# Decoding three steps of channel weights during the value projections of the second and third batch

## Chip, cores, metric

The kernel runs on one core of a Trainium2 chip. The metric is device time in microseconds (us) of one execution; the median of several executions counts.

## What is computed

Four batches of 448 positions pass through three stages: an attention whose weights are a sigmoid, a gated projection (value projection, a convolution over five positions as the gate, output projection), and a mixer that first mixes positions (`w_tok1`, `w_tok2`) and then channels (`w_ch1`, `w_ch2`).

```python
scores = scale * np.matmul(q, k.transpose(0, 1, 3, 2)) - np.log(S)   # q, k, v: (4, 12, 448, 64)
x = np.matmul(1.0 / (1.0 + np.exp(-scores)), v)                     # then (4, 448, 768)
gate = 1.0 / (1.0 + np.exp(-gate_pre))      # gate_pre: conv over 5 positions, by channel
x = gate * (x @ w_val) @ w_out              # (768, 768) each
h = np.maximum(x.transpose(0, 2, 1) @ w_tok1, 0.0) @ w_tok2          # (448, 256), (256, 448)
u = x + h.transpose(0, 2, 1)
out = u + np.maximum(u @ w_ch1, 0.0) @ w_ch2                         # (768, 1536), (1536, 768)
```

All weights arrive as float64. The program on the host only lays arrays out; turning a weight into something that TensorE can multiply happens on the chip and is called decoding below.

## The kernel before

**Precision.** Every dense product is made of three matmuls. A weight is decoded into a high and a low part (`decode_ops`, L91), an activation is split the same way (`split`, L75: a copy on ScalarE, a subtraction on VectorE), and high times high, low times high and high times low are summed in PSUM. Decoding 128x768 weights (a "piece") takes six VectorE instructions (L98, L105, L108, L113, L119, L122) and two ScalarE instructions (L101, L130) on a raw tile of 768 KB.

**Stages.** `lead` (L79 of the inner block) runs attention, with the decoding of `w_val`, `w_out`, `w_tok1` and `w_tok2` between. Then for each of the four batches `dense_steps(b)` gives the steps of the value projections (`val`, six of 18 matmuls each, L320), of output projections, transposes and the first half of the position mixing (`outs`), and of the second half (`t1`, `t2`). The second half of a batch is run among the value projections of the next one. Then the channel stage: it has twelve steps `fc` for every batch, each of 18 matmuls into `psh` (`ch1`, L641) and 18 into the six accumulators `pso` (`ch2`, L660), so that TensorE runs `ch1(b, fc)`, `ch2(b, fc - 1)`, `ch1(b, fc + 1)` and so on. Between the two a relu split (`r`: L76 on ScalarE, L78 on VectorE) turns `psh` into the operand of `ch2`.

**Channel weights.** Step `fc` needs two pieces, one of `w_ch1` and one of `w_ch2` (`ld_ch`, `ch_parts`). They are decoded once and stay for all batches. Step 0 has a place of its own in the pool `p2a`. Steps 1 to 3 (`CHAN_HELD = 4`) lie in the twelve `w` tiles that held `w_val`, which are free once the last value projection has run. Steps 4 to 11 lie in a pool `p2r` on the right side, where `w_out`, `w_tok1`, `w_tok2` and the tiles of the position mixing were. The raw tiles of these loads are two, reused in turn, and are loaded by the queue of SyncE.

**Order.** Until the end of the position mixing the order is written by hand. `weave(steps, ops, share)` runs TensorE's steps and puts small operations (`ops`) between them, spread over a share of the steps. In the last batch, step 0 is decoded among the value projections, and steps 1 to 3 (48 operations) together with six `prep_split` (the split of the input of the channel stage) among `outs`, `t1` and `t2`, over a share of 0.95 (`OS_SHARE`). What follows, the decoding of steps 4 to 11 and the channel stage, is put in order by the scheduler of the language; the decoding has a low priority (`CHAN_LOW`). On each engine instructions run in the order in which they stand, so an instruction that waits holds up those behind it.

**Other queues.** GpSimd's queue (POOL) carries the stores of `x2T` to device memory (`uscr`, L378) and small memsets (L274) at each `x_back`; SyncE's queue (SP) carries `x_back` (loads of `xb`), the loads of `u` from `uscr`, and the raw loads.

Of the kernel before, what the change touches and what calls it, by code (L numbers as in the profile page):

```python
# [9 lines left out]
F32 = mybir.dt.float32  # L10
F32R = mybir.dt.float32r
# [4 lines left out]


CHAN_HELD = 4
CHAN_LOW = 600
OS_SHARE = 0.95  # L20

# [6 lines left out]
def tile_kernel(ctx, tc, qT, kT, v, w_val, conv_w, w_out, w_tok1, w_tok2, w_ch1, w_ch2, out):  # L28
# [31 lines left out]
    dram = ctx.enter_context(tc.tile_pool(name="dram", bufs=1, space=bass.MemoryType.DRAM))  # L60
    uscr = dram.tile([B, KD, P, S], F32, name="uscr")
    xscr = dram.tile([NPT, P, S], F32, name="xscr")

    def f(ap):
        return ap.bitcast(F32)
# [22 lines left out]
        load(raw)  # L88
        return raw

    def decode_ops(pool, n, raw, h_out, l_out, sum_out=None):  # L91
        w = raw[:, : 2 * n].rearrange("p (n t) -> p n t", t=2)
        lo, hi = w[:, :, 0], w[:, :, 1]
        t = {}

        def first():
            t["a"] = pool.tile([P, DC], I32, tag="dec_a", bufs=2, name="dec_a")[:, :n]
            nc.vector.tensor_scalar(out=t["a"], in0=hi, scalar1=0x7FFFFE00, scalar2=None, op0=ALU.bitwise_and)  # L98

        def rebase():  # L100
            nc.scalar.activation(out=t["a"], in_=t["a"], func=AF.Relu, scale=8.0, bias=exp_b)  # L101

        def rest():
            t["c"] = pool.tile([P, DC], I32, tag="dec_c", bufs=1, name="dec_c")[:, :n]
            nc.vector.tensor_scalar(out=t["c"], in0=hi, scalar1=0x1FF, scalar2=None, op0=ALU.bitwise_and)  # L105

        def join():
            nc.vector.scalar_tensor_tensor(  # L108
                out=lo.bitcast(F32), in0=lo.bitcast(U32), scalar=2.0**-32, in1=t["c"], op0=ALU.mult, op1=ALU.add
            )  # L110

        def sign():
            nc.vector.scalar_tensor_tensor(  # L113
                out=t["a"], in0=hi, scalar=-0x80000000, in1=t["a"], op0=ALU.bitwise_and, op1=ALU.bitwise_or
            )

        def power():
            t["e"] = pool.tile([P, DC], I32, tag="dec_c", bufs=1, name="dec_e")[:, :n]
            nc.vector.tensor_scalar(out=t["e"], in0=t["a"], scalar1=-0x800000, scalar2=None, op0=ALU.bitwise_and)  # L119

        def low():
            nc.vector.scalar_tensor_tensor(  # L122
                out=l_out, in0=lo.bitcast(F32), scalar=2.0**-20, in1=t["e"].bitcast(F32), op0=ALU.mult, op1=ALU.mult
            )
# [35 lines left out]
    def w_tile():  # L160
        return wval.tile([P, DM], F32R, tag="w", bufs=2 * KD, name="w")
# [382 lines left out]
    def weave(steps, ops, share=0.85):  # L544
        total = int(share * sum(n for n, *_ in steps))
        count, at, done = len(ops), 0, 0
        for n, fn, *hold in steps:
            fn()
            at += n
            due = done if hold else min(count, count * at // total, done + 4)  # L550
            while done < due:
                ops[done]()
                done += 1
        for fn in ops[done:]:
            fn()
# [2 lines left out]
    wch_t, r_b = {}, []  # L558
    rp = {}

    def ld_ch(fc, which):
        raw = rp["a"].tile([P, 2 * DC], I32, tag="raw", bufs=2, name="raw")
        if which == 0:
            nc.sync.dma_start(
                raw.rearrange("p (k m) -> p k m", k=KD),
                w_ch1[:, fc * P : (fc + 1) * P].bitcast(I32).rearrange("(k p) m -> p k m", p=P),
            )
        else:
            nc.sync.dma_start(raw, w_ch2[fc * P : (fc + 1) * P].bitcast(I32))
        return raw  # L570


    def ch_parts(fc, which, raw):
        if which == 0:
            if 0 < fc < CHAN_HELD:
                wch[fc] = [[w_tile() for _ in range(2)] for _ in range(2)]
            else:
                t = wch_t.pop(fc)
                wch[fc] = [[t[:, n, a] for a in range(2)] for n in range(2)]
        return decode_ops(rp["a"], DM, raw, *wch[fc][which])  # L580

    def wch_alloc(pool, fc):
        wch_t[fc] = pool.tile([P, 2, 2, DM], F32R, name=f"wch{fc}")

    def dec_ch(fc):
        for which in range(2):
            for fn in ch_parts(fc, which, ld_ch(fc, which)):
                fn()

    def ch_ops(fcs):
        pieces = [(fc, which) for fc in fcs for which in range(2)]
        raws = {}

        def load(n):
            if n < len(pieces):
                raws[n] = ld_ch(*pieces[n])

        load(0)  # L600
        load(1)
        ops = []
        for n in range(len(pieces)):
            cur = []

            def op(k, n=n, cur=cur):
                if k == 0:
                    cur += ch_parts(*pieces[n], raws.pop(n))
                cur[k]()
                if k == 7:  # L610
                    load(n + 2)

            ops += [lambda k=k, op=op: op(k) for k in range(8)]
        return ops

    def prep_load(b, j):
# [53 lines left out]
    with tc.manual_schedule():  # L670
# [23 lines left out]
        for b in range(B):  # L694
            val, outs, t1, t2 = dense_steps(b)
            if b:
                weave(val[0] + back1 + sum(val[1:], []) + back2, first if b + 1 == B else [])
            else:
                val = sum(val, [])
                for n in (12, 8, 4):  # L700
                    val.insert(n, (0, dec_step))
                weave(val, [])
                assert not (begun or raws or decs)
                dec.release()
                dn["late"] = tc.alloc_tile_pool(name="late", bufs=1, side="right", reuse_waits="tile")
            if b + 1 < B:
                weave(outs, post_ops(b + 1))
            else:
                os = outs + t1 + t2
            back1, back2 = t1, t2  # L710
            if b + 2 == B:
                xbp.release()
                rp["a"] = tc.alloc_tile_pool(name="p2a", bufs=1, side="left")
                wch_alloc(rp["a"], 0)
                first = ch_ops((0,))
        for j in range(KD):
            prep_load(0, j)
        ops = ch_ops(range(1, CHAN_HELD))
        for j in range(KD):
            ops.insert(6 * j + 6, lambda j=j: prep_split(0, j))  # L720
        weave(os, ops, OS_SHARE)
        psw.release()
    pso = tc.alloc_tile_pool(name="pso", bufs=1, space=bass.MemoryType.PSUM, reuse_waits="tile")
# [5 lines left out]
    for fc in range(KF - 1, CHAN_HELD - 1, -1):  # L729
        wch_alloc(rp["p"], fc)  # L730
    r_b += [rp["p"].tile([P, 2, S], F32R, tag="r", bufs=2, name="r") for _ in range(2)]
    with tc.high_priority(-CHAN_LOW):
        for fc in range(CHAN_HELD, KF):
            dec_ch(fc)
    seq = [(b, fc) for b in range(B) for fc in range(KF)]
    order = []
# [55 lines left out]
```

## Time and profile before

| | us |
|---|---|
| median of three executions | 743.78 (743.14 to 745.97) |
| the profiled execution | 744.49 |
| its span, first to last instruction | 742.7 |
| TensorE (PE) busy | 732.5 |
| VectorE (DVE) busy | 399.3 |
| ScalarE (ACT) busy | 255.9 |
| GpSimd (POOL) busy | 26.5 |

The stages in the span: attention to about 133 us, the dense part of the four batches to about 376 us, the channel stage to the end. PE's busy time covers nearly all of the span, and its granted clock was 1.000 throughout. The profiled execution took 1.8 us more than its span, and 0.7 us more than the median of the runs. A row's idle time is the time an engine waited before an instruction, and the arrow names what ended the wait.

### The profile page before, as it was taken

What the parts mean: (1) busy time and instruction counts of PE and PEld (TensorE: products, weight loads), DVE (VectorE), ACT (ScalarE), POOL (GpSimd) and SP (SyncE); (2) the same over time, 40 slices, a digit from 0 to 9 for tenths busy, and PEclk for the clock granted to TensorE, in tenths of its full rate; (3) what the DMA queues carried; (4) which work ended last, traced back from release to release, by engine and by line L of the source; (5) the groups of instructions that cost most, each with busy time, mean ns of one, the idle gap of its engine ahead of it and who ended that gap; (6) DMA issues with size and microseconds to landing.
All of it is one profiled execution on the core that took longest, in us unless ns stands there. A gap on an engine that the chain in (4) does not pass through costs nothing.

```text
span 742.7 us, 10706 instructions
## 1 busy us (share of the span) xinstructions
PE 732.5 (99%) x4360; PEld 605.5 (82%) x4360; DVE 399.3 (54%) x690; ACT 255.9 (34%) x379; POOL 26.5 (4%) x66
## 2 busy tenths in 40 slices
PE   8999999999999999999999999999999999999997
PEld 3344444899999999999988987899999999999997
DVE  1899675589449548866799998811022101220102
ACT  6898888244214213323434443300020000200000
POOL 0001100000000100000010000000000000000000
PEclk9999999999999999999999999999999999999999
DMA  9858996201111101315265555510015000240002
GB/s 288 264 155 237 274 290 208 75 13 51 50 37 51 63 4 59 123 51 186 95 195 173 169 171 170 164 60 1 1 46 178 1 0 1 63 149 0 1 1 74
DMA packets 48864, 77.79 MB, mean 105 GB/s; under 512 B 4000, under 2 KB 44208, under 8 KB 48816
## 3 DMA queue, kind: packets, MB, share of 16 engines
q1 hardware_dynamic: 45168, 62.86, 27.8%
q0 software_dynamic: 3216, 13.80, 5.3%
q8 instruction: 34, 0.56, 0.3%
q10 hardware_dynamic: 432, 0.46, 0.2%
q14 instruction: 14, 0.11, 0.0%
HBM read 61.96 MB, written 15.14 MB: 104 GB/s over the span
## 4 chain that ended last, share of the span: by engine, by line
PE 84%; DVE 10%; DMA 4%; ACT 1%; issue 0%; SPq 0%; ACTq 0%
PE psd L320 24%; PE pso L660 18%; PE psh L641 18%; PE pss L242 8%; PE psy L257 8%; PE pst L360 4%; PE pst L373 3%; DMA raw<-w_ch 3%; DVE dec_a L113 2%; DVE raw L108 2%; DVE wch L122 2%; PE pst L343 1%; DVE dec_e L119 1%; DVE dec_a L98 1%; DVE dec_c L105 1%; ACT ga L244 1%
## 5 line engine op out<-in xcount | busy, mean ns | idle before, releaser
L78 DVE SCALAR_TENSOR_TENSOR r<-psh,r 128x448 fp32r<-128x448 f32 x48 | 29.8, 623 | 210.1 <-ACT r L76 210.1
L660 PE MATMUL pso<-r,wch 128*128 128x448 f32 x648 | 139.0, 367 | 2.5 <-DVE r L78 1.6
L641 PE MATMUL psh<-us,wch 128*128 128x448 f32 x648 | 139.3, 367 | 1.3 <-ACT wch L130 0.7
L660 PEld LDWEIGHTS pso<-r,wch 128*128 128x128 f32 x648 | 121.5, 188 | 13.9 <-DVE r L78 2.0
L641 PEld LDWEIGHTS psh<-us,wch 128*128 128x128 f32 x648 | 121.4, 188 | 13.7 <-ACT wch L130 1.6
L76 ACT ACTIVATE r<-psh 128x448 fp32r<-128x448 f32 x48 | 25.9, 542 | 225.1 <-PE psh L641 224.9
L320 PE MATMUL psd<-gv,w 128*128 128x448 f32 x432 | 92.4, 369 | 0.0
L244 ACT ACTIVATE ga<-pss,bias_s 128x896 f32<-128x896 f32 x84 | 83.4, 1003 | 19.2 <-PE pss L242 18.6
L320 PE MATMUL psd<-xs,w 128*128 128x448 f32 x432 | 88.8, 365 | 0.0
L320 PEld LDWEIGHTS psd<-xs,w 128*128 128x128 f32 x432 | 81.0, 188 | 7.0 <-issue 0.7
L320 PEld LDWEIGHTS psd<-gv,w 128*128 128x128 f32 x432 | 80.2, 188 | 6.7
L242 PE MATMUL pss<-q,k 64*64 64x448 f32 x672 | 78.4, 538 | 1.0 <-ACT ga L244 0.7
L257 PE MATMUL psy<-ga,v 64*64 64x448 f32 x672 | 77.6, 536 | 0.0
L290 DVE SCALAR_TENSOR_TENSOR gate<-xb,cw,gate 128x448 f32<-128x448 f32 x96 | 65.7, 684 | 2.8
L242 PEld LDWEIGHTS pss<-q,k 64*64 64x64 f32 x672 | 25.7, 133 | 39.7 <-issue 29.0
L257 PEld LDWEIGHTS psy<-ga,v 64*64 64x64 f32 x672 | 25.7, 133 | 37.4 <-issue 35.9
L101 ACT ACTIVATE dec_a<-dec_a,exp_b 128x768 int32<-128x768 int32 (+3 forms) x43 | 36.8, 866 | 45.3 <-DVE dec_a L98 45.3
L113 DVE SCALAR_TENSOR_TENSOR dec_a<-raw,dec_a 128x768 int32<-128x768 int32 (+2 forms) x42 | 37.2, 887 | 19.9 <-ACT dec_a L101 19.7
L641 PE MATMUL psh<-us,w 128*128 128x448 f32 x216 | 46.7, 367 | 0.0
L660 PE MATMUL pso<-r,w 128*128 128x448 f32 x216 | 46.2, 366 | 0.2 <-DVE r L78 0.2
L660 PEld LDWEIGHTS pso<-r,w 128*128 128x128 f32 x216 | 40.5, 188 | 4.0 <-DVE r L78 0.6
L641 PEld LDWEIGHTS psh<-us,w 128*128 128x128 f32 x216 | 40.6, 188 | 3.7
(69 smaller groups left out, 625.5 us busy)
## 6 DMA issues: line engine op xcount, KB each, us to landing
raw<-w_ch SPq DMA_DIRECT2D x24, 768.0 KB, 4.4
v<-v SPq DMA_DIRECT2D x24, 224.0 KB, 6.1
uscr<-x2T POOLq DMA_DIRECT2D x24, 224.0 KB, 2.6
u<-uscr SPq DMA_DIRECT2D x24, 224.0 KB, 3.5
ur<-uscr SPq DMA_DIRECT2D x24, 224.0 KB, 3.4
out<-ur SPq DMA_DIRECT2D x24, 224.0 KB, 2.1
q<-qT SPq DMA_DIRECT2D x23, 224.0 KB, 4.7
k<-kT SPq DMA_DIRECT2D x22, 224.0 KB, 4.7
```

The source lines that it names most:

```text
L76: nc.scalar.activation(out=h_out, in_=src, func=AF.Relu if relu else AF.Copy)
L78: nc.vector.scalar_tensor_tensor(out=l_out, in0=src, scalar=0.0, in1=f(h_out), op0=ALU.max, op1=ALU.subtract)
L101: nc.scalar.activation(out=t["a"], in_=t["a"], func=AF.Relu, scale=8.0, bias=exp_b)
L113: nc.vector.scalar_tensor_tensor(out=t["a"], in0=hi, scalar=-0x80000000, in1=t["a"], op0=ALU.bitwise_and, op1=ALU.bitwise_or)
L242: nc.tensor.matmul(ps[cols, j, :S], k[rows, keys], q[rows], start=True, stop=True)
L244: nc.scalar.activation(out=a, in_=ps[:, :, :S], func=AF.Sigmoid, bias=bias_s, scale=QK_SCALE)
L257: nc.tensor.matmul(y_t[i + h][cols, :S], v_t[i][rows, c, cols], a[rows, j], start=c == 0, stop=c == NB - 1)
L290: nc.vector.scalar_tensor_tensor(out=acc, in0=x[:, t : t + S], scalar=w, in1=acc, op0=ALU.mult, op1=ALU.add)
L320: nc.tensor.matmul(ps[:, :S], w(a, kk), s[:, c, :], start=kk == 0 and n == 0, stop=kk == KD - 1 and n == 2,)
L360: nc.tensor.matmul(ps[:, :HALF], a, x[:, m], start=n == 0, stop=n == len(mm) - 1)
L641: nc.tensor.matmul(ps[:, :S], wch[fc][0][a][:, kk * P : (kk + 1) * P], us_t[b, kk][:, c, :], start=kk == 0 and n == 0, stop=kk == KD - 1 a ...
L660: nc.tensor.matmul(acc[j][:, :S], wch[fc][1][a][:, j * P : (j + 1) * P], r[:, c, :], start=fc == 0 and n == 0, stop=fc == KF - 1 and n == 2,)
```

## The change

Three steps of channel weights, `PRE = (2, 3, 4)`, are no longer decoded where the others are. A pool `pre` on the left side, in the place of the attention tiles, is opened after the first batch's value projections. The six pieces are decoded in it, three beside the second batch's value projections and three beside the third's (27 operations in each `weave`, over a share of 0.95). A ninth operation of each piece (`keep`) stores the high and low part to a scratch tensor `wscr` in device memory, by GpSimd's queue. Where steps 2 and 3 were decoded, `pre_load` loads them from `wscr` into `w` tiles (eight loads of 384 KB), and step 4 into its place in `p2r` (four loads), all by GpSimd's queue. The last `weave` holds 22 operations instead of 54, and the scheduler's part decodes steps 5 to 11 instead of 4 to 11. In `pre` the tiles `dec_a`, `pre0` and `pre1` exist once.

```diff
+PRE = (2, 3, 4)
...
+    wscr = dram.tile([len(PRE), 2, 2, P, DM], F32, name="wscr")
...
+    def ch_parts(pool, fc, which, raw):
+        if fc in PRE:
+            to = [pool.tile([P, DM], F32R, tag=f"pre{a}", bufs=1, name="pre") for a in range(2)]
+            ops = decode_ops(pool, DM, raw, *to, bufs=1)
+            def keep():
+                for a in range(2):
+                    nc.gpsimd.dma_start(wscr[PRE.index(fc), which, a], f(to[a]))
+            return ops + [keep]
...
+    def pre_load(fc):
+        wch_place(fc)
+        for which in range(2):
+            for a in range(2):
+                nc.gpsimd.dma_start(wch[fc][which][a], wscr[PRE.index(fc), which, a])
...
             if b:
-                weave(val[0] + back1 + sum(val[1:], []) + back2, first if b + 1 == B else [])
+                weave(val[0] + back1 + sum(val[1:], []) + back2, first.pop(0), 0.95)
             else:
...
+                pre = tc.alloc_tile_pool(name="pre", bufs=1, side="left")
+                ops = ch_ops(pre, [(fc, which) for fc in PRE for which in range(2)])
+                first = [ops[: len(ops) // 2], ops[len(ops) // 2 :]]
...
             if b + 2 == B:
+                pre.release()
                 xbp.release()
                 rp["a"] = tc.alloc_tile_pool(name="p2a", bufs=1, side="left")
                 wch_alloc(rp["a"], 0)
-                first = ch_ops((0,))
+                first.append(ch_ops(rp["a"], [(0, 0), (0, 1)]))
         for j in range(KD):
             prep_load(0, j)
-        ops = ch_ops(range(1, CHAN_HELD))
+        ops = ch_ops(rp["a"], [(1, 0), (1, 1)])
+        for fc in PRE[:2]:
+            pre_load(fc)
         for j in range(KD):
-            ops.insert(6 * j + 6, lambda j=j: prep_split(0, j))
+            ops.insert(3 * j + 2, lambda j=j: prep_split(0, j))
         weave(os, ops, OS_SHARE)
...
+    pre_load(CHAN_HELD)
     with tc.high_priority(-CHAN_LOW):
-        for fc in range(CHAN_HELD, KF):
+        for fc in range(CHAN_HELD + 1, KF):
             dec_ch(fc)
```

How instructions stand on the engines is shown at three places. Line numbers of the changed kernel are 2 higher up to L380 (L331 is the L329 of before, L84 the L82, L379 the L377, L124 the L122, L80 the L78).

VectorE among the second batch's value projections, before: `gate` and `gv` are the product with the gate and the split behind each projection, `h` the relu split of the position mixing.

```order
L329 TENSOR_TENSOR gate<-psd,gate 128x448
L82 TENSOR_TENSOR gv<-gate,gv 128x448
L377 TENSOR_TENSOR x2T<-pst_2253,x2T 128x448
L377 TENSOR_TENSOR x2T<-pst_2262,x2T 128x448
L377 TENSOR_TENSOR x2T<-pst_2271,x2T 128x448
L288 TENSOR_SCALAR gate<-xb,cw 128x448
```

The same place in the changed kernel:

```order
L107 TENSOR_SCALAR dec_c<-raw 128x768
L110 SCALAR_TENSOR_TENSOR raw<-raw,dec_c 128x768
L115 SCALAR_TENSOR_TENSOR dec_a<-raw,dec_a 128x768
L331 TENSOR_TENSOR gate<-psd,gate 128x448
L84 TENSOR_TENSOR gv<-gate,gv 128x448
L121 TENSOR_SCALAR dec_e<-dec_a 128x768
L379 TENSOR_TENSOR x2T<-pst_2306,x2T 128x448
L124 SCALAR_TENSOR_TENSOR pre<-raw,dec_e 128x768
L379 TENSOR_TENSOR x2T<-pst_2319,x2T 128x448
L379 TENSOR_TENSOR x2T<-pst_2330,x2T 128x448
L290 TENSOR_SCALAR gate<-xb,cw 128x448
```

Three decode instructions stand ahead of the gate product and split of the last projection, and two more between it and the first gate convolution of the next batch.

VectorE at the end of the position mixing of the last batch, before: `r` is the relu split of the channel stage's first step, the last `x2T` rows free the PSUM banks that the channel stage needs.

```order
L113 SCALAR_TENSOR_TENSOR dec_a<-raw,dec_a 128x768
L119 TENSOR_SCALAR dec_e<-dec_a 128x768
L122 SCALAR_TENSOR_TENSOR w<-raw,dec_e 128x768
L78 SCALAR_TENSOR_TENSOR r_3720<-psh,r_3720 128x448
L98 TENSOR_SCALAR dec_a<-raw 128x768
L105 TENSOR_SCALAR dec_c<-raw 128x768
L108 SCALAR_TENSOR_TENSOR raw<-raw,dec_c 128x768
L377 TENSOR_TENSOR x2T<-pst_3729,x2T 128x448
L113 SCALAR_TENSOR_TENSOR dec_a<-raw,dec_a 128x768
L98 TENSOR_SCALAR dec_a<-raw 128x768
L119 TENSOR_SCALAR dec_e<-dec_a 128x768
L122 SCALAR_TENSOR_TENSOR w<-raw,dec_e 128x768
```

The same place in the changed kernel:

```order
L121 TENSOR_SCALAR dec_e<-dec_a 128x768
L80 SCALAR_TENSOR_TENSOR r_3792<-psh,r_3792 128x448
L124 SCALAR_TENSOR_TENSOR w<-raw,dec_e 128x768
L379 TENSOR_TENSOR x2T<-pst_3796,x2T 128x448
L379 TENSOR_TENSOR x2T<-pst_3805,x2T 128x448
L107 TENSOR_SCALAR dec_c<-raw 128x768
L379 TENSOR_TENSOR x2T<-pst_3815,x2T 128x448
L110 SCALAR_TENSOR_TENSOR raw<-raw,dec_c 128x768
L121 TENSOR_SCALAR dec_e<-dec_a 128x768
L100 TENSOR_SCALAR dec_a<-raw 128x768
L124 SCALAR_TENSOR_TENSOR wch_3841<-raw,dec_e 128x768
```

Between the relu split and the last `x2T` row stood more than a piece of decoding and stand now two instructions; `wch_3841`, the first half of step 5, follows at once.

GpSimd's queue from the last batch's value projections on, before and then in the changed kernel:

```order
L378 DMA uscr<-x2T 128x448 x12
```

```order
L380 DMA uscr<-x2T 128x448 x6
L601 DMA w<-wscr 128x768 x8
L380 DMA uscr<-x2T 128x448 x6
L601 DMA wch_3842<-wscr 128x768 x4
```

The loads of steps 2 and 3 stand behind the third batch's last stores, those of step 4 (`wch_3842`) behind the last batch's.

## Rows read from the trace of the kernel before

**Rows 1.** The page, busy time, share of the span and instructions of each engine.

```profile
PE 732.5 (99%) x4360; PEld 605.5 (82%) x4360; DVE 399.3 (54%) x690; ACT 255.9 (34%) x379; POOL 26.5 (4%) x66
```

**Rows 2.** Waits of PE, whole span: total us, times, longest.

```profile
PE pso L660 <- DVE r L78: 1.8, 2, 1.6
...
PE pso L660 <- DVE x2T L377: 0.8, 1, 0.8
...
PE psh L641 <- ACT wch L130: 0.7, 1, 0.7
PE psh L641 <- DVE us L82: 0.4, 1, 0.4
```

**Rows 3.** Timeline of PE: start, us, instruction, idle before it.

```profile
375.76 3.61 PE L641 MATMUL psh<-us,wch 128*128 128x448 f32 x17
...
392.82 3.31 PE L660 MATMUL pso<-r,wch 128*128 128x448 f32 x15 [0.84 <-DVE x2T L377]
...
445.41 0.47 PE L641 MATMUL psh<-us,wch 128*128 128x448 f32 x1 [0.66 <-ACT wch L130]
...
463.22 2.51 PE L660 MATMUL pso<-r,wch 128*128 128x448 f32 x11 [1.64 <-DVE r L78]
```

**Rows 4.** The chain that ended last, in order of time: start, us, what.

```profile
481.44 3.66 PE pso L660 x18
...
731.28 4.96 PE pso L660 x24
```

**Rows 5.** Stretches: length, busy of PE, PEld, DVE, ACT, POOL, clock, DMA share, GB/s.

```profile
200.00:210.00 10.00, 10.00 (x51) 9.27 (x50) 3.35 (x6) 1.23 (x3) 0.00 (x0) 1.00 0.01 2
...
420.00:430.00 10.00, 10.00 (x51) 9.23 (x50) 9.83 (x16) 4.25 (x6) 0.00 (x0) 1.00 0.56 190
```

**Rows 6.** The tile `raw`, 330 to 480 us: duration ns min/median/max.

```profile
L108 DVE SCALAR_TENSOR_TENSOR raw<-raw,dec_c x23: 949/959/962, 330.8 to 468.1; 128x768 f32<-128x768 uint32 x23
...
L98 DVE TENSOR_SCALAR dec_a<-raw x22: 548/555/562, 343.6 to 467.0; 128x768 int32<-128x768 int32 x22
...
DMA to landing us min/median/max: 4.1/4.4/7.8
```

**Rows 7.** Timeline of DVE in the channel stage.

```profile
395.59 0.96 DVE L122 SCALAR_TENSOR_TENSOR wch<-raw,dec_e 128x768 fp32r<-128x768 f32 x1
...
459.31 0.96 DVE L122 SCALAR_TENSOR_TENSOR wch<-raw,dec_e 128x768 fp32r<-128x768 f32 x1
462.07 0.56 DVE L98 TENSOR_SCALAR dec_a<-raw 128x768 int32<-128x768 int32 x1 [1.80 <-DMA raw<-w_ch]
```

**Rows 8.** Timeline of DVE, end of the second batch's value projections.

```profile
214.19 0.63 DVE L82 TENSOR_TENSOR gv<-gate,gv 128x448 fp32r<-128x448 f32 x1 [0.65 <-ACT gv L76]
...
217.17 0.44 DVE L288 TENSOR_SCALAR gate<-xb,cw 128x448 f32<-128x448 f32 x1
```

**Rows 9.** Timeline of PE there: the first and last matmuls of that stretch.

```profile
187.00 3.82 PE L320 MATMUL psd<-xs,w 128*128 128x448 f32 x18
...
216.43 5.74 PE L320 MATMUL psd<-gv,w 128*128 128x448 f32 x27
```

**Rows 10.** Timeline of DVE at the start of the last batch's output projections.

```profile
343.63 0.56 DVE L98 TENSOR_SCALAR dec_a<-raw 128x768 int32<-128x768 int32 x1 [3.05 <-DMA raw<-w_ch]
...
345.68 0.19 DVE L335 COPY x2T<-x2T 128x64 f32<-128x64 f32 x1 [1.03 <-ACT x2T L334]
```

**Rows 11.** Timeline of SP's queue: the raw load of step 1.

```profile
338.54 0.43 SPq L564 DMA_DIRECT2D raw<-w_ch  x1
```

**Rows 12.** DMA issues: count, KB each, median us to landing.

```profile
uscr<-x2T POOLq DMA_DIRECT2D x24, 224.0 KB, 2.6
...
raw<-w_out POOLq DMA_DIRECT2D x6, 768.0 KB, 7.4
```

**Rows 13.** Timeline of POOL.

```profile
340.87 0.54 POOL L378 DMA_DIRECT2D uscr<-x2T  x1 [0.70 <-DVE x2T L377]
...
392.53 1.35 POOL L378 DMA_DIRECT2D uscr<-x2T  x2 [3.40 <-DVE x2T L377]
```

More of the change, by code (lines that the diff above doesn't have):

```diff
@@ L89, in fetch, with decode_ops @@
         return raw
-    def decode_ops(pool, n, raw, h_out, l_out, sum_out=None):
+    def decode_ops(pool, n, raw, h_out, l_out, sum_out=None, bufs=2):
         w = raw[:, : 2 * n].rearrange("p (n t) -> p n t", t=2)
@@ L96, in first @@
         def first():
-            t["a"] = pool.tile([P, DC], I32, tag="dec_a", bufs=2, name="dec_a")[:, :n]
+            t["a"] = pool.tile([P, DC], I32, tag="dec_a", bufs=bufs, name="dec_a")[:, :n]
             nc.vector.tensor_scalar(out=t["a"], in0=hi, scalar1=0x7FFFFE00, scalar2=None, op0=ALU.bitwise_and)
@@ L559, in tile_kernel, with ld_ch @@
     rp = {}
-    def ld_ch(fc, which):
-        raw = rp["a"].tile([P, 2 * DC], I32, tag="raw", bufs=2, name="raw")
+    def ld_ch(pool, fc, which):
+        raw = pool.tile([P, 2 * DC], I32, tag="raw", bufs=2, name="raw")
         if which == 0:
@@ L570, in ld_ch, with wch_place @@
         return raw
-    def ch_parts(fc, which, raw):
-        if which == 0:
[L575 to L580, printed above, removed]
+    def wch_place(fc):
+        if 0 < fc < CHAN_HELD:
+            wch[fc] = [[w_tile() for _ in range(2)] for _ in range(2)]
+        else:
+            t = wch_t.pop(fc)
+            wch[fc] = [[t[:, n, a] for a in range(2)] for n in range(2)]
+    def ch_parts(pool, fc, which, raw):
[6 more added lines that the diff above has]
+            return ops + [keep]
+        if which == 0:
+            wch_place(fc)
+        return decode_ops(pool, DM, raw, *wch[fc][which])
+    def pre_load(fc):
+        wch_place(fc)
+        for which in range(2):
+            for a in range(2):
+                nc.gpsimd.dma_start(wch[fc][which][a], wscr[PRE.index(fc), which, a])
     def wch_alloc(pool, fc):
@@ L586, in dec_ch, with ch_ops @@
         for which in range(2):
-            for fn in ch_parts(fc, which, ld_ch(fc, which)):
+            for fn in ch_parts(rp["a"], fc, which, ld_ch(rp["a"], fc, which)):
                 fn()
-    def ch_ops(fcs):
-        pieces = [(fc, which) for fc in fcs for which in range(2)]
+    def ch_ops(pool, pieces):
         raws = {}
@@ L597, in load @@
             if n < len(pieces):
-                raws[n] = ld_ch(*pieces[n])
+                raws[n] = ld_ch(pool, *pieces[n])
         load(0)
@@ L607, in op @@
                 if k == 0:
-                    cur += ch_parts(*pieces[n], raws.pop(n))
+                    cur += ch_parts(pool, *pieces[n], raws.pop(n))
                 cur[k]()
@@ L611, in op @@
                     load(n + 2)
-            ops += [lambda k=k, op=op: op(k) for k in range(8)]
+            ops += [lambda k=k, op=op: op(k) for k in range(9 if pieces[n][0] in PRE else 8)]
         return ops
```

## The prediction

> **What bounds the kernel now.** I read the busy times first: PE is busy for 732.5 of 742.7 us and no other engine for much over half of the span [rows 1]. No matmul is removed, so the change can only win back time in which PE stands still. Second, PE's waits [rows 2]: the rows shown come to 3.7 us, and each names a decode instruction or an instruction that runs beside the decoding on VectorE or ScalarE. Third, their places [rows 3]: all lie between the start of the channel stage at 375.76 us and 463.22 us. In that stretch VectorE is full (9.83 us busy in 10), while among the value projections it is busy for 3.35 in 10 [rows 5].
>
> The waits understate the loss, since a broken row of matmuls also starts up more slowly. I count it by pace. From 481.44 us, where ch2 of the second batch begins, to 731.28 us, where the last 36 matmuls begin, are 34 steps of 36 matmuls [rows 4]: 249.84 / 34 = 7.35 us a step, 0.204 us a matmul. Between 375.76 [rows 3] and 481.44 us lie 14 ch1 and 12 ch2 of 18 matmuls and 18 matmuls of the position mixing, 486 in all, or 13.5 steps: 99.2 us at the pace. They took 105.7. **So 6.5 us is what PE loses there, and the most that the change can give.** The upper bound of the gain is this 6.5, the lower bound for "all waits gone" the 3.7 of the rows.
>
> **The change, part by part.**
>
> *Removed from the last stretch.* Six pieces leave it. A piece has three VectorE instructions of about 0.95 us (L108; L113 and L122 are of the same kind and shape) and three of about 0.55 (L98, likewise L105 and L119) [rows 6]: 3 x 0.95 + 3 x 0.55 = 4.5 us. Four of the six, steps 2 and 3, go out of the last weave: 18 us of VectorE's work. Two, step 4, go out of the scheduler's part: 9 us.
>
> *What that does to the early waits.* The wait on x2T at 392.82 us [rows 3] comes from VectorE being behind: between the relu splits of the first half's position mixing and the last x2T row stood 20 decode instructions, and now nine. The PSUM bank that PE waited for should be free at about 384 us, and PE asks for it at 375.76 + 54 x 0.204 = 386.8 us. The wait on `us` goes for the same reason: all six splits stand ahead of the relu split of the first step.
>
> *What it does to the late waits.* Here VectorE runs a race with PE. Before, the first half of step 4 was ready at 396.55 us and the 14th piece (second half of step 10) at 460.27 [rows 7]: 63.7 / 13 = 4.9 us a piece, relu splits and waits for raw loads included. A step of PE takes 7.35 us and needs two pieces, 9.8, so decoding falls behind by 2.45 us a step and the lead it starts with decides. In the changed kernel the first piece of this kind is that of step 5; from the order I put its end at about 388 us (the last x2T row at 384, then a wait for the second raw tile, which is issued when the piece before is done with it, at about 381.6, plus 4.4 [rows 6], then 1.5 us of instructions). The 14th and last piece is then ready at 388 + 13 x 4.9 = 451.7 us. PE without waits begins ch1 of step k at 383.1 + 7.35 (k - 1): step 11 at 456.6, and its piece, the 13th, is ready at 446.8, ten us early. Tighter are the relu splits, since they stand among the pieces in VectorE's order: that of step 9 stands behind four instructions of the last piece, ready at about 450.2, and PE wants it for ch2 at 452.9. That leaves 2.7 us; one raw load as late as the one at 462.07 us (1.80 us of VectorE's waiting) [rows 7] fits in, two don't. I leave 0.5 us of waits in the sum for this.
>
> *Added beside the value projections.* 18 VectorE instructions, 3 x 4.5 = 13.5 us, in each of two stretches of 216.43 - 187.00 = 29.4 us [rows 9], in which VectorE had some two thirds free [rows 5]. That fits, if narrowly, and the question is the end: the split `gv` of the last projection. It ended at 214.8 us before [rows 8]; with L107, L110 and L115 ahead of it I put it at 215.3. PE needs it at the 16th matmul after 216.43 us, at 219.5 [rows 9]: 4.2 us to spare. The convolutions behind it begin 1.3 us later than at 217.17 [rows 8], and VectorE's next wait takes that up. ScalarE gets two instructions a piece and has nine tenths free there. Cost: nothing; the cover is these 4.2 us. The six raw loads on SP's queue stand ahead of x_back loads that are not due yet, in a stretch where the DMA queues are nearly empty (0.01 of their time) [rows 5]. The 12 stores stand on POOL's queue ahead of memsets and stores that nobody on PE waits for soon.
>
> *The loads back.* Steps 2 and 3: eight loads on POOL, behind the store at 340.87 us [rows 13], needed from 390 us on. The nearest rows bound one load of 384 KB between 2.6 us (224 KB stored) and 7.4 us (768 KB loaded) [rows 12]; even one after the other at 6 us they are there by 390. Step 4: four loads behind the last x2T row, so from about 384 us; PE needs two of them at 383.1 + 3 x 7.35 = 405.2 and two at 416. One after the other at the dear end, 2 x 7.4 = 14.8, they are there at 399. Nothing on POOL stands behind them. What they do cost is DMA time beside the raw loads of step 5: their 1.5 MB can delay a raw load by some 3 us at this place, where decoding still has its whole lead.
>
> *Sum.* Gain 6.5 - 0.5 = 6.0 us. The profiled execution took 744.49: 738.5. It lies 0.7 above the median of the runs, 743.78, from which it would be 737.8. I say **738.0**.
>
> **Rivals.**
>
> *The race is lost again.* The raw loads are slowed by the loads of step 4 for longer, or VectorE starts step 5 later than I think. For: loads took up to 7.8 us instead of 4.4 [rows 6], and the relu split of step 9 has 2.7 us. If both raw tiles of step 5 take twice as long (2 x 4.4 = 8.8 us of delay), PE waits for 8.8 - 2.7 = 6.1 us and the gain is gone: 744. Against: the two first steps are decoded far ahead of PE, so a delay of one tile only eats lead. Time: 740.5 to 744.5, with waits on `r` late in the first batch.
>
> *Slower: the loads back block the transposes.* L100 of step 1 stands on VectorE ahead of the copy of x2T that PE's first transposes need. The raw tile was issued at 338.54 us [rows 11], L98 began at 343.63, and the copy came at 345.68 after ScalarE [rows 10]; PE wants the transposes at about 347, so L98 must begin by 346.5. The eight new loads begin at 341.4, 3.1 MB beside this tile. If the tile takes turns with them at the dear rate it lands at 338.5 + 2 x 7.4 = 353.3 and PE waits 7 us: 745. If it is served last, 3.9 MB at 768 KB in 7.4 us [rows 12] take 37 us, it lands at 375 and PE waits 28: 766. It decides from a landing after 346.5 + 6.0 + 3.7 = 356 us on. Against: the tile was issued 3 us earlier and had all but landed.
>
> *Slower: GpSimd's issues are held up.* POOL issued two stores in 1.35 us at 392.53 [rows 13], in a stretch where VectorE had no gap, and a single one took 0.54. If it could only issue in VectorE's gaps, 0.17 us in 10 [rows 5], the first two loads of step 4, 1.08 us, would need 64 us from 384 on, 448 instead of 405: 43 us slower, 781. The Trainium skill, "SBUF — State Buffer", section "SBUF: two separate sides", speaks for such a lock: while VectorE runs an operation that uses the port pair it shares with GpSimd, the descriptors of a DMA that GpSimd issues cannot be written, and the DMA waits. By that rule the change should have used another queue; the trace disagrees as far as it goes, with issues of 0.54 us in the densest stretch.
>
> *The value projections don't hide it.* If waits between VectorE and ScalarE in the single `dec_a` cost over 4.2 us more than I walked, twice, PE waits for the rest: 740 to 748.
>
> **How the numbers follow.** A measurement of this kernel can tell about 0.5%, 3.7 us: faster is below 740.1, slower above 747.5. Chances: the forecast 0.74 (737 to 740); the race lost again 0.17 (mostly 740.5 to 744.5, a quarter of it still faster); blocked transposes 0.04; held issues 0.02; no cover 0.03 (half the same). Faster: 0.74, less 0.03 for its own edge, plus 0.04, is 0.75. Slower: 0.04 + 0.02 and a little, 0.06. Same: the rest, 0.19. The range begins at 743.78 - 6.9 (13.5 steps at 7.32, two halves of 3.66 [rows 4], are 98.8) = 736.8, and reaches to 741.8, the nearer third of the lost race.
>
> **What would show it.** Right: no wait on L379 or `us` between 376 and 393 us of the changed profile; ch1 and ch2 in unbroken rows of 18 with 7.35 us a step from the first step of the channel stage; VectorE near 8 in 10 among the second and third value projections and PE without waits there; the last piece decoded near 452 us; the loads of step 4 landed before 400. Wrong: waits of PE on `r` from 430 us on (the race), a wait on transposes near 347 (blocked), on `wch` at 405 (held issues), or on `gv` at 219 and 281 us (no cover).

## The result

The changed kernel takes **738.87 us** (median of six executions, 738.64 to 739.55). Six executions of the kernel before on the same chip gave 744.88 us (743.05 to 747.26). The ratio is 0.9919, with an interval of 0.9895 to 0.9943: 6.0 us or 0.8% faster, against a forecast of 738.0 us and 6.0 us. The spread of the times fell too, from 4.2 to 0.9 us.

The profiled execution took 739.55 us, its span is 737.7 us (742.7 before), and the granted clock was 1.000, that is 2.4 GHz, throughout. The page of the changed kernel answers to [rows 1]; its second line gives the shares of the chain that ended last, by engine:

```profile
PE 730.6 (99%) x4360; PEld 607.1 (82%) x4360; DVE 398.1 (54%) x690; ACT 256.4 (35%) x379; POOL 41.0 (6%) x90
...
PE 97%; DMA 1%; DVE 1%; ACT 1%; issue 0%; SPq 0%; ACTq 0%
```

PE does the same 4360 matmuls, and VectorE the same 690 instructions: work was moved, not saved. GpSimd's 24 more instructions are the 12 stores and 12 loads. Now 97% of the chain is PE, where it was 84% before.

The waits of PE in the whole span, total us, times and longest, answer to [rows 2]:

```profile
PE pss L244 <- DMA k<-kT: 1.5, 2, 0.9
PE psi L703 <- DVE zero L692: 1.2, 1, 1.2
PE pss L244 <- ACT ga L246: 0.5, 2, 0.4
```

All of them lie in the first 30 us, at the start of the attention. No wait on `r`, `x2T`, `wch` or `us` is left. The timeline of PE through the channel stage (start, us, instruction) answers to [rows 3]:

```profile
377.15 3.81 PE L661 MATMUL psh<-us,wch 128*128 128x448 f32 x18
...
439.48 3.81 PE L680 MATMUL pso<-r,wch 128*128 128x448 f32 x18
...
454.16 3.81 PE L680 MATMUL pso<-r,wch 128*128 128x448 f32 x18
...
476.33 3.82 PE L680 MATMUL pso<-r,wch 128*128 128x448 f32 x18
```

The rows are whole, 18 matmuls each. The last one shown is the first ch2 of the second batch. From 377.15 to 476.33 us is **99.18 us**, which is the 99.2 us that the prediction worked out for this stretch without waits. Before, the first of the two stands at 375.76 us [rows 3], and the same view has the second at 481.27 us, 105.51 us later:

```profile
481.27 3.82 PE L660 MATMUL pso<-r,wch 128*128 128x448 f32 x18
```

The stretch gave 6.33 us. Below, "the stretch" always means the distance between these two matmuls in the timeline.

The span gained less, 5.0 us, because in this execution the channel stage began 1.4 us later (377.15 against 375.76). The profiles of step4, step2, extra, alias, spload and crowd begin it at 376.1 to 376.5, that of steps23 at 377.0. 0.9 us of the 1.4 is a longer wait for the first keys, and 0.56 us stands in the first batch's value projections, which the change does not touch. The medians, 6.0 us apart, don't rest on one start.

### The profile page after: what moved, and what is told of

Its sections match the earlier page's. It is cut to its first block, busy times and chain, and to the rows that moved or that the text cites. A ratio compares the mean times of both kernels' runs of the same rounds, so it can differ in the third digit from the quotient of the medians.

```text
span 737.7 us, 10749 instructions
## 1 busy us (share of the span) xinstructions
PE 730.6 (99%) x4360; PEld 607.1 (82%) x4360; DVE 398.1 (54%) x690; ACT 256.4 (35%) x379; POOL 41.0 (6%) x90
## 4 chain that ended last, share of the span: by engine, by line
PE 97%; DMA 1%; DVE 1%; ACT 1%; issue 0%; SPq 0%; ACTq 0%
PE psd L322 24%; PE psh L661 24%; PE pso L680 24%; PE psy L259 8%; PE pss L244 8%; PE pst L362 4%; PE pst L375 4%; PE pst L345 1%; DMA k<-kT 1%; ACT ga L246 0%; DMA out<-ur 0%; DVE ur L687 0%; DVE dec_a L115 0%; DVE w L124 0%; ACT dec_a L103 0%
## 5 line engine op out<-in xcount | busy, mean ns | idle before, releaser
L80 DVE SCALAR_TENSOR_TENSOR r<-psh,r 128x448 fp32r<-128x448 f32 x48 | 29.9, 623 | 218.2 <-ACT r L78 218.2
L78 ACT ACTIVATE r<-psh 128x448 fp32r<-128x448 f32 x48 | 26.0, 542 | 234.3 <-PE psh L661 234.2
```

What stands on the lines that cost most here:

```text
L80: nc.vector.scalar_tensor_tensor(out=l_out, in0=src, scalar=0.0, in1=f(h_out), op0=ALU.max, op1=ALU.subtract)
```

## Experiments

The gain of each kernel is the difference from the median of the kernel before, measured beside it on the same chip: 744.88 us for the changed kernel, 745.31 for steps23, step2, step4 and extra, 745.13 for alias, beside2, spload and crowd, 745.59 for steps2345. These medians of one kernel differ by 0.7 us, so times of different groups are compared by gain and by stretch; each stretch is from one profiled execution.

| kernel | median us | gain us | ratio (interval) | stretch us |
|---|---|---|---|---|
| changed kernel | 738.87 | 6.0 | 0.9919 (0.9895 to 0.9943) | 99.18 |
| steps23 | 738.77 | 6.5 | 0.9912 (0.9894 to 0.9929) | 99.18 |
| step2 | 740.00 | 5.3 | 0.9930 (0.9912 to 0.9947) | 99.64 |
| step4 | 741.19 | 4.1 | 0.9945 (0.9928 to 0.9963) | 101.34 |
| extra | 745.07 | 0.2 | 0.9994 (0.9982 to 1.0007) | |
| alias | 738.20 | 6.9 | 0.9910 (0.9891 to 0.9929) | 98.99 |
| spload | 738.80 | 6.3 | 0.9917 (0.9900 to 0.9934) | 99.17 |
| crowd | 739.29 | 5.8 | 0.9927 (0.9909 to 0.9945) | 99.48 |
| beside2 | 752.69 | -7.6 | 1.0106 (1.0088 to 1.0125) | 99.18 |
| steps2345 | 744.04 | 1.6 | 0.9979 (0.9960 to 0.9999) | 102.77 |

### What is gained by which step: steps23, step4, step2

The list of steps decoded early is cut. The steps left out are decoded where the kernel before decodes them, so that the last `weave` and the scheduler's part follow the list. The places of the six `prep_split` follow its length: `6 * j + 6` in step4, as in the kernel before, and `5 * j + 4` in step2.

```diff
-PRE = (2, 3, 4)
+PRE = (2, 3)      # steps23; (4,) in step4, (2,) in step2
...
-        ops = ch_ops(rp["a"], [(1, 0), (1, 1)])
-        for fc in PRE[:2]:
-            pre_load(fc)
+        ops = ch_ops(rp["a"], [(fc, which) for fc in range(1, CHAN_HELD) if fc not in PRE for which in range(2)])
+        for fc in PRE:
+            if fc < CHAN_HELD:
+                pre_load(fc)
...
-        for fc in range(CHAN_HELD + 1, KF):
-            dec_ch(fc)
+        for fc in range(CHAN_HELD, KF):
+            if fc not in PRE:
+                dec_ch(fc)
```

> Steps 2 and 3 alone are decoded early, step 4 is decoded in the channel stage as in the kernel before. Theory (a race between decoding and PE, decided by the lead that decoding starts with): the last weave is that of the changed kernel, so the waits of PE on x2T and us go, and the first piece of step 4 should be ready near 388 us instead of 396.55. The race then ends early enough by a microsecond or two: gain 5.0 to 6.5 us against the kernel before, within 1.5 us of the changed kernel, no wait of PE over 0.5 us in the first batch of the channel stage. Rival (every step of weights that leaves the last stretch gives its third): gain 2/3 of 6, 4.0 us.

steps23 has the whole gain. Its stretch is 99.18 us, and PE waits for nothing in it. Step 4 adds nothing that these runs show once steps 2 and 3 are out of the last `weave`, and the changed kernel moves half as much traffic again for it. It even costs slack: the tightest relu split, that of step 7, ends 2.2 us before PE needs it in the profile of steps23 and 0.4 us in that of the changed kernel (worked out below). That every step is worth a third of the gain falls.

> Step 4 alone is decoded early, the last weave decodes steps 1 to 3 as in the kernel before. Theory: the early waits of PE (on us at 380 us and x2T at 392, with the slow restarts 2.4 us of the 6.5) stay, the late ones (from 437 us on, 4.1 us) go, since decoding begins with step 5 about where it began with step 4: gain 3.5 to 4.5 us against the kernel before. Rival (each step gives its third): gain 2.0 us.

step4 keeps all of the last `weave` and takes two pieces off the race. Its waits of PE in the stretch:

```profile
PE pso L680 <- DVE x2T L379: 0.9, 1, 0.9
PE psh L661 <- DVE us L84: 0.4, 1, 0.4
PE pso L680 <- DVE r L80: 0.2, 1, 0.2
```

The early waits of [rows 2], on `x2T` and `us`, stand as they did, and the late ones, 1.6 us on `r` and 0.7 on `wch`, are gone. The stretch loses 2.16 us to the pace. This splits the 6.3 us: about 2.2 belong to the early waits and about 4.2 to the race, each with what the broken rows lose beside their waits. It also explains steps23: VectorE's backlog when the channel stage starts is the cause of both, so taking work out of the last `weave` cures both, and taking it out of the race alone cures the race.

> Step 2 alone is decoded early; the last weave decodes steps 1 and 3, the scheduler's part steps 4 to 11. Theory: the early waits fall from 2.4 us to under 1, the first piece of step 4 is ready near 391 us, 5 us earlier than before, and the race is lost by 1 to 3 us instead of 4.1: gain 3 to 5 us. Rival (each step gives its third): gain 2.0 us. A rival by which any wait of VectorE on a raw load moves one for one into PE: gain 0 to 2.

Two pieces out of the last `weave` give 5.3 us, a little over what was expected and 1.2 us more than the two pieces of step 4. The intervals of the two overlap; their stretches are 1.7 us apart. The stretch loses 0.46 us, with no wait recorded in it, where 1 to 3 us of a lost race had been expected. So the first two pieces bring most, and two pieces taken out of the last `weave` bring more than two taken out of the race.

### What the added work costs: extra, alias

The kernel before, and beside it the early decoding and the stores; nothing is loaded back, and steps 2 to 4 are decoded again where they were:

```diff
+                pre = tc.alloc_tile_pool(name="pre", bufs=1, side="left")
+                pres[0] = pre
+                ops = ch_ops(pre, [(fc, which) for fc in PRE for which in range(2)])
+                first = [ops[: len(ops) // 2], ops[len(ops) // 2 :]]
...
-        ops = ch_ops(range(1, CHAN_HELD))
+        ops = ch_ops(rp["a"], [(fc, which) for fc in range(1, CHAN_HELD) for which in range(2)])
```

> The kernel before with the added work alone: the six pieces of steps 2 to 4 are loaded, decoded beside the second and third value projections and stored to device memory, but nothing reads them, and all steps are decoded where they were. Theory: the value projections hide it whole, 0 us against the kernel before (within 1), and PE waits nowhere between 187 and 290 us. Rival (part of the gain is paid back there): 1 to 4 us slower than before, with waits of PE on gv or psd near 219 and 281 us.

Six more pieces, 27 us of VectorE's work, cost nothing that can be measured: 0.9994 (0.9982 to 1.0007). The busy times in extra's first stretch among the second batch's value projections (columns as in [rows 5]):

```profile
200.00:210.00 10.00, 10.00 (x51) 9.27 (x50) 8.10 (x13) 3.47 (x5) 0.97 (x2) 1.00 0.55 183
```

VectorE is busy for 8.10 in 10 where it was 3.35, and PE still for 10.00. Its waits in the channel stage are those of [rows 2] again, among them 1.7 us on `r` and 0.9 on `x2T`.

alias takes the opposite side: the early decoding, the stores and the loads are left out, and steps 2 to 4 multiply by step 1's weights.

```diff
-                ops = ch_ops(pre, [(fc, which) for fc in PRE for which in range(2)])
-                first = [ops[: len(ops) // 2], ops[len(ops) // 2 :]]
+                first = [[], []]
...
-        for fc in PRE[:2]:
-            pre_load(fc)
...
-    pre_load(CHAN_HELD)
+    for fc in PRE:
+        wch[fc] = wch[1]
```

> Leaves out the decoding of steps 2, 3 and 4 altogether: no early decoding, no stores, no loads back, and these steps multiply by the weights of step 1. It is the changed kernel without any cost of the early decoding. Theory (all of the added work is hidden and no wait of PE is left in the channel stage): the same time as the changed kernel, 738.4 to 739.4. Rival (the added work or the loads back still cost something): 1 to 3 us less than the changed kernel.

738.20 us, 0.7 under the changed kernel and 0.2 under what was expected; the two intervals overlap widely. By the medians the work that the change adds costs 0.7 us, by the gains 0.9 and by the stretches 0.2, and whether it costs anything isn't settled. Little more is left to win from this loss: with the work gone for good the gain is 6.9 us.

### Whether the cover can be exceeded: beside2

All six pieces beside the second batch, none beside the third:

```diff
-                first = [ops[: len(ops) // 2], ops[len(ops) // 2 :]]
+                first = [ops, []]
```

> All six pieces are decoded beside the second batch's value projections, none beside the third's. Theory (the cover there is VectorE's free time plus some 4 us at the end): 27 us of decoding beside 10.4 us of its own work and 4 us of waiting in 29.4 us is 41 us, 12 too many; less the slack PE waits some 5 to 8 us on gv near 219 us, and the time is 743.5 to 747. Rival (PSUM banks and the later stages take the lag up): under 2 us over the changed kernel.

752.69 us, 7.6 us slower than before. The sign and the place came as expected, but the time lies over 5 us beyond the expected range. PE's largest wait, and its timeline at the last two projections:

```profile
PE psd L322 <- ACT gv L78: 7.6, 2, 5.0
```

```profile
222.84 1.13 PE L322 MATMUL psd<-gv,w 128*128 128x448 f32 x3 [2.51 <-ACT gv L78]
...
229.02 6.97 PE L322 MATMUL psd<-gv,w 128*128 128x448 f32 x21 [5.05 <-ACT gv L78]
235.83 0.49 PE L345 MATMUL pst<-ident,x2T 128*128 128x128 f32 x3
```

Six pieces are 27 us of work, and VectorE was busy for 12.9 of these 29.4 us already in the kernel before (the 10.4 of the expectation comes from one stretch of 10 us); so the splits of the last projections came late. PE's waits on `gv` are within the 5 to 8 us that were expected, but two things were not in the sum, so that this agreement is partly luck. First, `pre` exists once, so VectorE had to wait until a store had left it. Three such waits, 2.41, 0.86 and 1.20 us, make 4.5 us; the timeline of DVE shows the first:

```profile
203.86 0.96 DVE L124 SCALAR_TENSOR_TENSOR pre<-raw,dec_e 128x768 fp32r<-128x768 f32 x1 [2.41 <-DMA wscr<-pre]
```

Second, the clock. The stretches of beside2:

```profile
210.00:220.00 10.00, 10.00 (x50) 8.87 (x48) 7.78 (x13) 3.13 (x5) 1.63 (x3) 1.00 0.51 161
220.00:230.00 10.00, 2.44 (x8) 1.31 (x7) 7.16 (x12) 3.75 (x5) 1.84 (x3) 0.71 0.67 236
230.00:240.00 10.00, 9.22 (x38) 8.08 (x37) 9.76 (x17) 4.28 (x8) 3.04 (x6) 0.78 0.40 147
```

The granted clock is 0.71 of 2.4 GHz in the stretch in which PE was busy for only 2.44 of 10 us, and 0.78 in the next. Read in steps of 2 us it is 1.00 up to 224 us, 0.50 (the lower level of 1.2 GHz) from 226 to 234, and 1.00 again from 236 on. Before it fell, PE had done three matmuls since 220.3 us; before it rose, PE had been busy without a break since 229.0. The 21 matmuls from 229.02 us to 235.83 took 0.324 us each instead of 0.204, 2.5 us more. Two waits behind them, on `x2T` and `x`, add 1.7 us. With the 7.6 us on `gv` these are 11.8 of the 13.0 us by which the span is longer than that of the changed kernel. The channel stage then runs its stretch in 99.18 us as in the changed kernel; the whole loss lies ahead of it.

### The loads back: spload, crowd

spload issues the loads back on SP's queue instead of GpSimd's:

```diff
-                nc.gpsimd.dma_start(wch[fc][which][a], wscr[PRE.index(fc), which, a])
+                nc.sync.dma_start(f(wch[fc][which][a]), wscr[PRE.index(fc), which, a])
```

> The changed kernel with the loads back issued by SP's queue instead of GpSimd's. Theory (issues and landings on GpSimd's queue are early enough, and nobody on PE waits for them): the same time, 738.4 to 739.8, and a load of 384 KB lands in about the 7 to 9 us that it took on GpSimd's queue at these places. Rival (GpSimd's issues are held up beside VectorE): the loads land 2 us or more sooner after their issue; the time can't show it where PE has no wait, but the lead in the race would.

The same time, 738.80 us, and the same stretch, 99.17 us. The DMA issues (count, KB each, median us from issue to landing), of the changed kernel and then of spload:

```profile
w<-wscr POOLq DMA_DIRECT2D x8, 384.0 KB, 8.6
wch<-wscr POOLq DMA_DIRECT2D x4, 384.0 KB, 7.3
```

```profile
w<-wscr SPq DMA_DIRECT2D x8, 384.0 KB, 9.2
wch<-wscr SPq DMA_DIRECT2D x4, 384.0 KB, 8.2
```

Counted from their issue they land no sooner. Nor are the issues on GpSimd's queue held up, as its timeline (POOL) in the changed kernel shows:

```profile
343.31 2.80 POOL L601 DMA_DIRECT2D w<-wscr  x5
...
386.10 2.69 POOL L601 DMA_DIRECT2D wch<-wscr  x4
```

Four issues in 2.69 us, 0.67 each, between 386.10 and 388.79 us, in a stretch in which VectorE (third number) was busy for 8.41 of 10 us:

```profile
380.00:390.00 10.00, 10.00 (x51) 9.27 (x50) 8.41 (x14) 2.58 (x5) 4.57 (x7) 1.00 0.70 210
```

VectorE stood idle for 1.36 us of just this time, so the 12 stores of the early decoding say more: they were issued in 0.54 us each, beside a VectorE that was busy for 7.85 and 8.29 of 10 us. A lock that holds GpSimd's DMAs up beside the decoding isn't seen. The Trainium skill, "SBUF — State Buffer", section "SBUF: two separate sides", has a DMA that GpSimd issues wait while VectorE holds their shared port pair, and advises another queue; in the changed kernel no issue of the loads took over 0.89 us, and whether the decode instructions hold that pair no run here shows.

The other queue does give something that the time can't show, and the expectation had named it: lead. The raw-load wait of spload's race, its relu split of step 7 and PE's ch2 of that step, from the timelines of DVE and PE:

```profile
387.07 0.56 DVE L100 TENSOR_SCALAR dec_a<-raw 128x768 int32<-128x768 int32 x1 [1.05 <-DMA raw<-w_ch]
...
432.18 0.62 DVE L80 SCALAR_TENSOR_TENSOR r<-psh,r 128x448 fp32r<-128x448 f32 x1
```

```profile
438.76 3.81 PE L680 MATMUL pso<-r,wch 128*128 128x448 f32 x18
```

VectorE waits for raw tiles for 1.05 us in this race, where it waits for 5.2 in the changed kernel, and the split of step 7 ends 6.0 us before its ch2 begins, where it ends with it there. On SP's queue the loads of step 4 don't stand behind the stores that wait for the last `x2T` rows: they begin 6.4 us after the start of the channel stage instead of 9.0, and no raw load behind them takes over 6.9 us, where one took 8.5. The last piece is ready 2.0 us earlier, counted from the start of the stage. The rest of the 6.0 us is order, since in spload the split of step 7 also stands about one piece earlier among VectorE's instructions; what each is worth alone was not tried.

crowd lengthens the transfers beside the first raw loads of the race. Behind the four loads of step 4, and as each of them has landed, it stores the same 1.5 MB to a scratch tensor that nobody reads:

```diff
     pre_load(CHAN_HELD)
+    for which in range(2):
+        for a in range(2):
+            nc.gpsimd.dma_start(wspare[which, a], f(wch[CHAN_HELD][which][a]))
```

> The changed kernel, and behind the four loads of step 4 the same 1.5 MB are stored to an unused place in device memory, so that the DMA traffic beside the raw loads of steps 5 to 7 doubles. Theory (the relu splits of the first batch have almost no slack left in the changed kernel: that of step 7 ended at 439.47 us and PE began with it at 439.48): a further delay of the raw loads by 2 to 4 us goes into PE, 740 to 743, with waits on r. Rival (the lead absorbs it): 738.4 to 739.5 and no wait.

739.29 us: 0.4 more than the changed kernel, under what was expected and in the range of the rival; the difference is within the noise, and the profile lists no wait on `r`. The added traffic made VectorE wait for raw tiles for 5.6 us (0.88, 4.07, 0.19 and 0.42) instead of 5.2 (1.36, 3.31 and 0.55), 0.3 us more, where 2 to 4 had been expected. Yet PE lost a little at once. The relu split of step 7 in crowd's timeline of DVE, and PE's ch2 of that step:

```profile
438.65 0.62 DVE L81 SCALAR_TENSOR_TENSOR r<-psh,r 128x448 fp32r<-128x448 f32 x1
```

```profile
438.62 4.21 PE L681 MATMUL pso<-r,wch 128*128 128x448 f32 x18
442.67 2.61 PE L662 MATMUL psh<-us,wch 128*128 128x448 f32 x12
```

The split ends at 439.27 us, 0.65 us after ch2 of step 7 began, and these 18 matmuls take 4.05 us to the next row, where 3.65 is usual. The changed kernel has next to nothing to spare at this place.

### One step more: steps2345

Four steps early, four pieces beside each batch, and eight loads behind the last `x2T` row instead of four (the edit of steps23 with another list):

```diff
-PRE = (2, 3, 4)
+PRE = (2, 3, 4, 5)
```

> Four steps, 2 to 5, are decoded early: four pieces beside each of the second and third batch's value projections, and eight loads instead of four behind the last x2T row. Theory of the cover: in the changed kernel the last gv split ends at 216.71 us and PE wants it at about 220.9, 4.2 us of slack; the fourth piece takes 4.5 us of VectorE, and the single pre tiles may add a wait for a store, so PE waits 0.3 to 3 us on gv in each of the two batches, and no wait is left in the channel stage to win back: 739.5 to 744. Rival (three steps were too few, a fourth helps): under 738.4. Rival (the eight loads slow the raw loads of step 6 and the race is lost): waits on r after 400 us, 739.5 to 742, and none on gv.

744.04 us, only 1.6 us faster than before and just past the far edge of what was expected (744): most of the gain is gone at four steps. None of the three cases came as stated: there is no wait on `gv`, and waits on `r` come together with a loss beside the value projections. Against the changed kernel the span is 5.5 us longer, 3.6 in the stretch and 1.9 ahead of it. Why the stretch loses is seen in the timelines of DVE and PE:

```profile
403.67 0.56 DVE L100 TENSOR_SCALAR dec_a<-raw 128x768 int32<-128x768 int32 x1 [6.84 <-DMA raw<-w_ch]
```

```profile
405.75 0.68 PE L680 MATMUL pso<-r,w 128*128 128x448 f32 x2 [0.90 <-ACT r L78]
407.15 3.52 PE L680 MATMUL pso<-r,w 128*128 128x448 f32 x16 [0.73 <-DVE r L80]
...
445.27 3.51 PE L680 MATMUL pso<-r,wch 128*128 128x448 f32 x16 [0.66 <-DVE r L80]
```

A raw load beside eight loads back holds VectorE up for 6.84 us instead of 3.31. The relu split of step 2 stands behind it, and PE, with its weights there long ago, waits for the split; the last row is ch2 of step 7. The decoding beside the value projections shows its end as well: not at `gv`, but where the convolutions have fallen behind, with two waits at the start of the next position mixing:

```profile
PE pst L362 <- DVE x L348: 1.7, 2, 1.0
```

## Why the prediction was right, and where it was off

**The bound and the loss.** PE's idle time in this one stretch was all there was to win. It was put at 6.5 us; by one view alone it is 6.3, since the prediction took the end from the chain of waits (481.44) [rows 4] and the start from the timeline [rows 3], and the two views date the same matmul 0.17 us apart. The pace of 99.2 us was met to a few hundredths. That the medians lie 6.0 us apart, the forecast to a tenth, is partly luck: the interval of the ratio is 4.2 to 7.8 us, and the 0.5 us left for waits came out as zero. The time came out 0.9 us above the forecast because 738.0 was counted in the main from 743.78, the median of three executions, where six gave 744.88.

**The early waits.** Right: in the changed kernel neither `x2T` nor `us` is waited for. step4 shows that they hang on the last `weave`, as the prediction said, and that they and their restarts were worth some 2.2 us.

**The race.** The mechanism was right, and this is where the sizes were off. The late raw loads, their landing times, and the race's last instructions in the changed kernel's timeline of DVE:

```profile
388.10 0.56 DVE L100 TENSOR_SCALAR dec_a<-raw 128x768 int32<-128x768 int32 x1 [1.36 <-DMA raw<-w_ch]
...
398.06 0.56 DVE L100 TENSOR_SCALAR dec_a<-raw 128x768 int32<-128x768 int32 x1 [3.31 <-DMA raw<-w_ch]
...
407.75 0.56 DVE L100 TENSOR_SCALAR dec_a<-raw 128x768 int32<-128x768 int32 x1 [0.55 <-DMA raw<-w_ch]
...
438.86 0.61 DVE L80 SCALAR_TENSOR_TENSOR r<-psh,r 128x448 fp32r<-128x448 f32 x1
...
452.96 0.62 DVE L80 SCALAR_TENSOR_TENSOR r<-psh,r 128x448 fp32r<-128x448 f32 x1
...
454.08 0.96 DVE L124 SCALAR_TENSOR_TENSOR wch<-raw,dec_e 128x768 fp32r<-128x768 f32 x1
```

```profile
DMA to landing us min/median/max: 4.2/4.4/8.5
```

The first piece of step 5 was ready at 389.5 us and the last at 455.0, where 388 and 451.7 had been said. The channel stage began 1.4 us later in this profile, so the true lateness is near zero at the start and 1.9 us at the end: (455.04 - 389.54) / 13 is 5.04 us a piece instead of 4.9. The raw load issued at 389.56 us, beside the four loads of step 4, took 8.5 us and cost VectorE 3.31; "some 3 us" had been said for it. But the prediction let that delay eat lead and did not subtract it from the slack of the relu splits. **That term was mis-sized**: 2.7 us for step 9, whose split ends at 453.58 us, 0.6 ahead of its ch2 at 454.16. The tightest split is that of step 7, and it ends at 439.47 us. Its ch2 begins at 439.48 and needs the low half from its third matmul on (the row of steps2345 breaks there), at 439.48 + 2 x 0.204 = 439.89. The slack is 0.4 us. crowd shows it from the other side: counted from the start of the channel stage its split ends 0.7 us later, and PE loses 0.4. So by this kernel's profile the rival "the race is lost again" lay nearer than its 0.17 said, although what it would have cost at first is small. spload shows that the place of the loads in GpSimd's queue and the order that went with it used up this slack. The 0.5 us left for waits came out as zero.

**Beside the value projections.** Right in what it costs, but one reading was too kind: that VectorE had two thirds free there was taken from one stretch of 10 us [rows 5]. Over the whole 29.4 us it was busy for 12.9 before, and for 23.3 in the changed kernel. The stretches of the changed kernel (columns as in [rows 5]), and the end of the second batch's projections in the timelines of DVE and PE:

```profile
200.00:210.00 10.00, 10.00 (x51) 9.28 (x50) 7.85 (x13) 3.41 (x5) 0.01 (x1) 1.00 0.56 153
210.00:220.00 10.00, 10.00 (x51) 9.17 (x50) 8.29 (x14) 3.30 (x5) 2.21 (x4) 1.00 0.43 163
```

```profile
216.08 0.63 DVE L84 TENSOR_TENSOR gv<-gate,gv 128x448 fp32r<-128x448 f32 x1 [0.64 <-ACT gv L78]
```

```profile
217.83 7.60 PE L322 MATMUL psd<-gv,w 128*128 128x448 f32 x36
```

VectorE is near 8 in 10, and PE is full. The last split ends at 216.71, and PE needs it at the 16th matmul, 217.83 + 15 x 0.204 = 220.9 us: 4.2 us to spare, as worked out. extra shows no cost that can be measured, and beside2 that the cover ends between three pieces and six.

**The loads back.** Right. Step 4 had landed by about 396 us (issued until 388.8, 7.3 us to landing at the median); PE asks for the first of it at 406.4. The transposes were not held up: in the changed kernel L100 began at 345.43 us after a wait of 2.94 us, the copy of `x2T` at 345.90 (345.68 before [rows 10]), and PE shows no wait there. The dear end of 7.4 us for a load was a little short: the eight and the four, issued close behind one another, took 8.6 and 7.3 us at the median.

**Rivals.** Held issues: not seen, at 0.67 us an issue, and step 4 had landed ten us before it was asked for. (The 0.54 us that the prediction placed in the densest stretch is the store at 340.87 us; in the dense one two took 1.35, 0.68 each [rows 13].) Blocked transposes: not seen. No cover: not seen at three pieces a batch, and real at six, with a price of 13.0 us of span against the changed kernel (750.7 against 737.7), where the prediction's case, up to 748 us, had neither the waits on the one `pre` tile nor the clock in it. What the prediction didn't see is that step 4 need not have been moved at all: the 9 us taken out of the race and the 18 us taken out of the last `weave` were counted as one sum, where the 18 alone do (steps23).

## What to carry to other kernels

Where one engine feeds another in a race, the lead at the start decides: find the stretch in which the feeder falls behind and empty that one, since work taken out ahead of it counts for every step behind. The slack of such a race lies in the small instructions that stand between the large ones in the feeder's queue, so check each of them, with the delay of the loads already taken off. And move no more than the stall needs, as moved work has a cover of its own that ends abruptly, and its transfers land in the race they were meant to help.

## What was not expected of the hardware

A raw load beside four loads back kept VectorE waiting for 3.31 us, one beside eight for 6.84 (steps2345); the same 1.5 MB again, stored once the four loads had landed, lengthened all such waits together by 0.3 us (crowd). So the delay went with what was under way when the raw load was issued; in spload, where the four loads had begun 2.6 us earlier, no raw load of the race took over 6.9 us instead of 8.5. Whether the direction of the transfer matters too was not tried.

In beside2 the clock was still at 0.78 of 2.4 GHz in the stretch in which PE was busy again for 9.22 in 10: this idle stretch of PE cost more than its own length, 2.5 us on top for 21 matmuls.

The changed kernel, steps23 and spload repeat within 0.9 us and alias within 1.3, while the kernels that wait in the stretch spread wider (step4 1.9, steps2345 2.6, extra 2.8, before 4.2). But step2 (2.0), crowd (1.7) and beside2 (1.9) list no wait there either, and extra and steps2345 were executed twice as often. So the spread alone does not tell whether the race is won, and what sets it stays open.
